# Two small jobs change engines: the columns of ones of the reused weight tiles, and the first chunk's casts

## The chip, the cores and the metric

The kernel runs on one core of a Trainium2 chip. A core has five engines with a queue each: TensorE (PE in the profile, with its weight loads as PEld), VectorE (DVE), ScalarE (ACT), GpSimd (POOL) and SyncE (SP), which here only issues transfers. They run beside each other and meet through semaphores. The metric is the time of one execution in microseconds (us), the median of several runs.

## The reference

Four batches of eight heads, 768 tokens, head width 64. Queries and keys are hashed by six random projections into 64 buckets, and a query attends only to keys of its own bucket. The heads' outputs, side by side, are the 512-wide rows of a feed-forward layer with three branches of which the largest value is kept.

```python
q_bits = (np.einsum('bhsd,dk->bhsk', q, proj) > 0).astype(np.int64)
k_bits = (np.einsum('bhsd,dk->bhsk', k, proj) > 0).astype(np.int64)
...
mask = q_bucket[:, :, :, None] == k_bucket[:, :, None, :]
scores = scale * np.matmul(q, k.transpose(0, 1, 3, 2))
scores = np.where(mask, scores, -1000000000.0)
scores = scores - np.max(scores, axis=-1, keepdims=True)
attn = np.exp(scores)
attn = attn / (np.sum(attn, axis=-1, keepdims=True) + 1e-09)
...
x = np.ascontiguousarray(attn_out.transpose(0, 2, 1, 3)).reshape(B * S, H * D)
...
h = np.maximum(np.maximum(x @ w1, x @ w2), x @ w3)
return (h @ w_out).astype(np.float32)
```

Inputs and outputs are float32.

## The kernel before

**Chunks and units.** The queries of a batch are cut into chunks: three of 256 queries in the first batch, two of 384 in each of the others, nine in all. A unit is one step of the attention: for one chunk and one head, as many blocks of 128 keys as give 768 score columns, so three blocks of 256 queries in the first batch and two of 384 later. Each batch has 48 units, the kernel 192. For a unit TensorE computes scores from S, a tile with the scaled heads and, below them, the hash bits as plus or minus one half (L299). ScalarE then takes one exponential over all 768 columns (L307) into a weight tile AT; its bias lets only equal hashes through. The scores lie in one of two buffers in PSUM, so TensorE can start the scores of a unit only when the exponential of the unit two before it has ended.

**Weight tiles.** There are 29 AT tiles, handed out first in, first out (`at_free`). A tile holds its blocks side by side, and behind each block's columns stand two columns of ones, which let the matmul with the values give the sum of the values as one column more. Their place depends on the block's width: the tiles start in the 256-wide form, with ones written by VectorE (L531). When a unit of the second batch takes a tile that is still in that form, `scores` lets VectorE write the new ones in front of the exponential:

```python
        if at_form[i] != w:
            nc.vector.memset(t[:, :, w : w + 2], 1.0)
            at_form[i] = w
```

That is L305. Tiles that the first batch's chunks give back for heads 4 to 7 (`i == 1`) have theirs written by GpSimd when they are given back (L396), at the end of a burst.

**Bursts.** When four heads of a chunk are done, a burst multiplies the weights with a matrix of ones (L359, the sums) and with the values (L381, one matmul group for each half of the value columns), with transposes and a reciprocal of the sums on VectorE (L366 to L370) and the scaled result into the chunk's xT (L388). From the fourth chunk on, VectorE first adds the blocks (L330, L333) and the sums of eight heads are taken at once (L414).

**Feed-forward groups.** When a chunk's xT is whole, its feed-forward work is put in a list and handed out one piece for each unit, behind that unit's scores: a group of four matmuls (L447) for one of three branches and one of six column blocks. The first branch's result is cast out of PSUM into ht by ScalarE (L451); the other two are folded in by VectorE with a maximum (L453). In the first chunk all six casts come first, in six groups one after another; in later chunks a cast comes with every third group. At the end come the output matmuls (L488) and their copies by ScalarE (L492). All these, the hash and the bursts share four PSUM banks, taken and given back in turn.

**Preparation.** The heads of the later batches are transposed on VectorE in blocks of 32 (L203), narrowed by GpSimd (L208), and written into S by transfers that SP issues (L213); their hash is computed by TensorE (L222), turned into bits by VectorE (L225) and sent to S by SP (L233). GpSimd also issues transfers: weights (L249, wout in L246), values (L241), and heads (L197).

**Order.** Nothing is rearranged: each engine executes its instructions in the order in which the program issues them. One loop over the units issues in each turn the scores of the next unit, the preparation that is planned for that turn (`when`), a piece of feed-forward work if there is credit, and the bursts that are due. The memset of L305 is issued with the scores, so on VectorE it stands behind everything of the turns before.

Of the kernel before, what the change touches and what calls it, by code (L numbers as in the profile page):

```python
# [17 lines left out]
def kernel(  # L18
# [12 lines left out]
    nc = tc.nc  # L31
# [59 lines left out]
    def bank():  # L91
        i = free_banks.pop(0)
        return i, bank_tiles[i]

    def give(i):
        if i is not None:
            free_banks.append(i)
# [168 lines left out]
    UPB = NU // B  # L266
# [4 lines left out]
    at_free = list(range(NAT))  # L271
    at_form = [THIRD] * NAT
    at_of = {}
# [6 lines left out]
    def block_of(b, m):  # L280
        return 2 * (m % MH) + m // MH if b == 0 else m
# [29 lines left out]
    def weights_of(c, h, m):  # L311
        w = chunks[c][2]
        nb = 2 * HALF // w
        return blocks(at_tiles[at_of[unit_at[c, h, m // nb]]], w)[:, m % nb, :]

    def xt_of(c):
        if c not in xts:
            xts[c] = x_pool.tile([P, NJC, HALF], FP16, tag="xT", name="xT")
        return xts[c]
# [15 lines left out]
    def sum_blocks(c, h):  # L335
        w = chunks[c][2]
        if (c, h) in sum_of:
            t = sum_of[c, h]
            return [t[:, j, 0:w] for j in range(1 if c >= THIRD_ADD else 2)]
        return [weights_of(c, h, m)[:, 0:w] for m in range(NM)]  # L340

    def burst(c, i):
        b, q0, w = chunks[c]
        held = {}
        rb = []

        def own_bank(key):
            if c == NCH - 1 and i == 1 and key != 1:
                return None, sc_ps.tile([P, 2, 512], FP32, tag="sc", name="sc")[:, 0, :]
            return bank()  # L350

        def sums(m0, m1):
            if m0 == 0:
                held["s"] = own_bank("s")
            sm = held["s"][1]
            bs = [sum_blocks(c, 4 * i + x) for x in range(4)]
            for m in range(len(bs[0])):
                for x in range(4):
                    nc.tensor.matmul(sm[Q * x : Q * (x + 1), 0:w], ones[:, :], bs[x][m],  # L359
                                     start=(m == 0), stop=(m == len(bs[0]) - 1))  # L360
            if m1 == NM:
                ys = ys_pool.tile([P, HALF], FP32, tag="ys", name="ys")
                rr = small.tile([P, HALF // Q], FP32, tag="rr", name="rr")
                n = w // Q
                rb.append(rb_pool.tile([P, HALF], FP32, tag="rb", name="rb"))
                nc.vector.transpose(ys[:, 0:w], sm[:, 0:w])  # L366
                give(held["s"][0])
                nc.vector.tensor_scalar(out=rr[:, 0:n], in0=ys[:, 0:w:Q], scalar1=EPS * S, scalar2=None, op0=AluOp.add)
                nc.vector.reciprocal(rr[:, 0:n], rr[:, 0:n])
                nc.vector.transpose(rb[0][:, 0:w], rr[:, 0:n].unsqueeze(2).to_broadcast((P, n, Q)))  # L370

        def values(side, m0, m1):
            if m0 == 0:
                held[side] = own_bank(side)
            av = held[side][1]
            first = (b, i, side) not in sv_of
            n = w + 1 if first else w
            for m in range(m0, m1):
                cb = block_of(b, m)
                for x in range(4):  # L380
                    nc.tensor.matmul(av[Q * x : Q * (x + 1), 0:n], v_at[2 * b + i][:, x, cb * D + side : (cb + 1) * D : 2],  # L381
                                     weights_of(c, 4 * i + x, m)[:, 0:n], start=(m == 0), stop=(m == NM - 1))
            if m1 == NM:
                if first:
                    sv_of[b, i, side] = small.tile([P, 1], FP32, tag=f"sv{side}", name="sv")
                    nc.vector.tensor_scalar(out=sv_of[b, i, side][:], in0=av[:, w : w + 1], scalar1=EPS, scalar2=None,
                                            op0=AluOp.mult)
                nc.vector.scalar_tensor_tensor(out=xt_of(c)[:, 2 * i + side, 0:w], in0=av[:, 0:w],  # L388
                                               scalar=sv_of[b, i, side][:], in1=rb[0][:, 0:w], op0=AluOp.add, op1=AluOp.mult)
                give(held[side][0])  # L390
                if side == 1:
                    for h in range(4 * i, 4 * i + 4):
                        for n in range(parts_of(c)):
                            a = at_of[unit_at[c, h, n]]
                            if b == 0 and i == 1:
                                nc.gpsimd.memset(blocks(at_tiles[a], HALF)[:, :, HALF : HALF + 2], 1.0)  # L396
                                at_form[a] = HALF
                            at_free.append(a)

        return sums, values, rb  # L400


# [33 lines left out]
    def ffn_groups(c):  # L436
        b, q0, w = chunks[c]
        xt = xt_of(c)
        hts, gs, l2 = {}, [], {}
        jobs = [(fb, wi) for fb in range(NFB) for wi in range(3)]  # L440
        if c == 0:
            jobs = [(fb, wi) for wi in range(3) for fb in range(NFB)]
        for fb, wi in jobs:
            def go(fb=fb, wi=wi):
                k_, ps = bank()
                for jc in range(NJC):
                    nc.tensor.matmul(ps[:, 0:w], w_sb[wi][:, jc, fb * P : (fb + 1) * P], xt[:, jc, 0:w],  # L447
                                     start=(jc == 0), stop=(jc == NJC - 1))
                if wi == 0:
                    hts[fb] = h_pool.tile([P, HALF], FP16, tag="ht", name="ht")  # L450
                    nc.scalar.copy(hts[fb][:, 0:w], ps[:, 0:w])  # L451
                else:
                    nc.vector.tensor_tensor(out=hts[fb][:, 0:w], in0=hts[fb][:, 0:w], in1=ps[:, 0:w], op=AluOp.max)  # L453
                give(k_)
            gs.append(go)
        rows = out[b * S : (b + 1) * S, :].rearrange("(p c) m -> c p m", c=NM)

        def out_rows(tb):
            if c < NCH - 1:
                return o_pool.tile([P, DM], FP32, tag="osb", name="osb")  # L460
            if "end" not in nat:
                nat["end"] = nat_pool.tile([P, 4 * NM * D], FP32, tag="nat", name="nat")
            return nat["end"][:, tb * DM : (tb + 1) * DM]

        def last(tb, cs, use_act):
            k_, ps = bank()
            n = cs.stop - cs.start
            for fb in range(NFB):
                nc.tensor.matmul(ps[:, 0:n], hts[fb][:, tb * P : (tb + 1) * P], wout_sb[:, fb, cs],  # L469
                                 start=(fb == 0), stop=(fb == NFB - 1))  # L470
            osb = out_rows(tb)
            if use_act:
                nc.scalar.copy(osb[:, cs], ps[:, 0:n])
            else:
                nc.vector.tensor_copy(osb[:, cs], ps[:, 0:n])
            give(k_)
            (nc.scalar if use_act else nc.sync).dma_start(rows[block_of(b, q0 // P + tb)][:, cs], osb[:, cs])

        def item(tb, part):
            def go2(part, tb=tb):  # L480
                if c == NCH - 1 and tb == w // P - 1:
                    last(tb, slice(part * DM // 2, (part + 1) * DM // 2), part == 0)
                    return
                if part == 0:
                    l2[tb] = bank()
                k_, ps = l2[tb]
                for fb in range(part * MH, (part + 1) * MH):
                    nc.tensor.matmul(ps[:, 0:DM], hts[fb][:, tb * P : (tb + 1) * P], wout_sb[:, fb, :],  # L488
                                     start=(fb == 0), stop=(fb == NFB - 1))
                if part == 1:  # L490
                    osb = out_rows(tb)
                    nc.scalar.copy(osb[:, 0:DM], ps[:, 0:DM])  # L492
                    give(k_)
                    nc.sync.dma_start(rows[block_of(b, q0 // P + tb)], osb[:, 0:DM])
            gs.append(lambda: go2(part))

        ntb = w // P
        steps = [(0, 0)]
        for tb in range(1, ntb):
            steps += [(tb, 0), (tb - 1, 1)]  # L500
        steps.append((ntb - 1, 1))
        if c == NCH - 1:
            steps = steps[:-3] + [steps[-2], steps[-3], steps[-1]]
        for tb, part in steps:
            item(tb, part)
        return gs
# [202 lines left out]
```

## Time and profile before

| What | Value |
|---|---|
| Median of 3 runs | 265.15 us (264.85 to 265.51) |
| The profiled execution | 264.99 us, of which 262.8 us from the first to the last instruction |
| TensorE, matmuls | 256.1 us busy, 97% |
| VectorE | 199.2 us busy, 76% |
| ScalarE | 180.7 us busy, 69% |
| GpSimd | 69.9 us busy, 27% |
| L305, memsets of ones on VectorE | 5, 62 ns each, from 55.5 to 62.2 us |
| L396, memsets of ones on GpSimd | 24, 102 ns each, from 41.1 to 60.7 us |
| L451, casts on ScalarE | 54: 18 of 128x256 (401 ns), 36 of 128x384 (481 ns) |

Times of instructions are counted from the first instruction of the profiled execution. In a row of a group, the line number and the engine come first, then what is written and read with its shape; behind the bar stand the total busy time, the mean duration of one in ns, and the idle time of the engine just before these instructions with what ended it. In a timeline row the start and the duration come first. Instructions of one engine overlap in part, so a row's duration is longer than its share of the engine's time. TensorE's ends are modelled.

### The profile page before, as it was taken

What the parts mean: (1) busy time and instruction counts of PE and PEld (TensorE: products, weight loads), DVE (VectorE), ACT (ScalarE), POOL (GpSimd) and SP (SyncE); (2) the same over time, 40 slices, a digit from 0 to 9 for tenths busy, and PEclk for the clock granted to TensorE, in tenths of its full rate; (3) what the DMA queues carried; (4) which work ended last, traced back from release to release, by engine and by line L of the source; (5) the groups of instructions that cost most, each with busy time, mean ns of one, the idle gap of its engine ahead of it and who ended that gap; (6) DMA issues with size and microseconds to landing.
All of it is one profiled execution on the core that took longest, in us unless ns stands there. A gap on an engine that the chain in (4) does not pass through costs nothing.

```text
span 262.8 us, 6491 instructions
## 1 busy us (share of the span) xinstructions
PE 256.1 (97%) x2503; PEld 155.8 (59%) x2503; DVE 199.2 (76%) x472; ACT 180.7 (69%) x276; POOL 69.9 (27%) x132
## 2 busy tenths in 40 slices
PE   7999999999999999999999999999999999999995
PEld 3655657765675676556555555556555555555552
DVE  3897757567598799769989899799847895888360
ACT  3797876765999199935898278981898739581322
POOL 3868753274067017400162412110000000000000
PEclk9999999999999999999999999999999999999999
DMA  7996999979446826950064851900230003000303
GB/s 216 339 243 141 173 238 225 204 158 219 143 113 185 159 64 111 240 159 12 0 180 122 163 94 40 199 4 18 59 121 2 0 2 120 2 1 2 120 0 120
DMA packets 20717, 30.95 MB, mean 118 GB/s; under 512 B 2608, under 2 KB 15248, under 8 KB 20688
## 3 DMA queue, kind: packets, MB, share of 16 engines
q0 software_dynamic: 8128, 13.37, 26.7%
q1 hardware_dynamic: 12128, 16.66, 21.7%
q10 hardware_dynamic: 432, 0.52, 0.6%
q8 instruction: 19, 0.31, 0.5%
q14 instruction: 10, 0.08, 0.1%
HBM read 25.17 MB, written 6.29 MB: 120 GB/s over the span
## 4 chain that ended last, share of the span: by engine, by line
PE 90%; ACT 7%; issue 1%; DVE 0%; ACTq 0%
PE ms L447 34%; PE sc L299 23%; PE ms L381 11%; PE ms L488 11%; ACT AT L307 5%; PE ms L222 3%; PE ms L359 2%; PE ms L124 1%; PE ms L538 1%; PE ms L172 1%; PE ms L414 1%; ACT ht L451 1%; PE ms L151 1%; PE ms L469 1%; PE sc L381 0%
## 5 line engine op out<-in xcount | busy, mean ns | idle before, releaser
L307 ACT ACTIVATE AT<-sc 128x768 f16<-128x768 f32 x192 | 153.1, 822 | 55.7 <-PE sc L299 52.7
L447 PE MATMUL ms<-xT,w_sb 128*128 128x384 f16 (+1 forms) x648 | 115.0, 308 | 0.2 <-DVE xT L388 0.2
L299 PE MATMUL sc<-S 72*128 72x384 bf16 (+1 forms) x432 | 93.7, 308 | 1.9 <-ACT AT L307 1.3
L447 PEld LDWEIGHTS <-w_sb 128*128 128x128 f16 x648 | 62.8, 97 | 35.6
L453 DVE TENSOR_TENSOR ht<-ht,ms 128x384 f16<-128x384 f16 (+1 forms) x108 | 54.2, 504 | 34.4 <-PE ms L447 21.9
L299 PEld LDWEIGHTS <-S 72*128 72x128 bf16 (+1 forms) x432 | 39.9, 98 | 32.2 <-issue 11.4
L208 POOL TENSOR_SCALAR T<-T 128x768 bf16<-128x768 f32 x24 | 22.8, 952 | 85.1 <-issue 51.5
L488 PE MATMUL ms<-wout_sb,ht 128*128 128x512 f16 x138 | 35.5, 378 | 0.0
L381 PE MATMUL ms<-AT,vo 128*32 128x385 f16 (+3 forms) x840 | 33.4, 308 | 0.0
L451 ACT CAST ht<-ms 128x384 f16<-128x384 f32 (+1 forms) x54 | 24.5, 454 | 8.8 <-PE ms L447 8.8
L381 PEld LDWEIGHTS <-vo 128*32 128x32 f16 x864 | 23.6, 96 | 8.5 <-issue 1.3
L330 DVE TENSOR_TENSOR ad<-ad,AT 128x768 f16<-128x768 f16 x48 | 26.9, 560 | 2.2 <-ACT AT L307 1.5
L330 DVE TENSOR_TENSOR ad<-AT,AT 128x768 f16<-128x768 f16 x48 | 27.7, 578 | 0.2 <-ACT AT L307 0.2
L203 DVE STREAM_TRANSPOSE T<-nat 128x384 f32<-128x384 f32 x48 | 26.5, 562 | 0.0
L488 PEld LDWEIGHTS <-ht 128*128 128x128 f16 x138 | 13.3, 97 | 13.0 <-issue 0.3
L388 DVE SCALAR_TENSOR_TENSOR xT<-ms,sv,rb 128x384 f16<-128x384 f32 (+1 forms) x35 | 19.1, 563 | 1.1
L492 ACT COPY osb<-ms 128x512 f32<-128x512 f32 x21 | 12.3, 588 | 6.1 <-issue 5.0
L333 DVE TENSOR_TENSOR ad<-ad 128x384 f16<-128x384 f16 x32 | 15.5, 484 | 1.1
L138 POOL TENSOR_SCALAR S<-T 64x384 bf16<-64x384 f32 (+1 forms) x23 | 14.1, 616 | 4.7 <-DVE T L133 3.1
L197 POOL DMA_DIRECT2D nat<-in_q_dram x20 | 11.1, 559 | 0.5 <-issue 0.4
L177 DVE TENSOR_SCALAR S<-ms 6x384 bf16<-6x384 f32 x16 | 8.9, 554 | 2.0 <-PE ms L172 1.2
L197 POOL DMA_DIRECT2D nat<-in_k_dram x16 | 9.0, 570 | 0.4
(60 smaller groups left out, 109.9 us busy)
## 6 DMA issues: line engine op xcount, KB each, us to landing
out_dram<-osb SPq DMA_DIRECT2D x21, 256.0 KB
S<-T SPq DMA_DIRECT2D x48, 96.0 KB
nat<-in_q_dram POOLq DMA_DIRECT2D x20, 192.0 KB, 5.9
vo<-in_v_dram POOLq DMA_DIRECT2D x8, 384.0 KB, 7.8
nat<-in_k_dram POOLq DMA_DIRECT2D x16, 192.0 KB, 4.2
w_sb<-in_moe_w_dram POOLq DMA_DIRECT2D x3, 768.0 KB, 10.2
nat<-in_k_dram SPq DMA_DIRECT2D x10, 192.0 KB
nat<-in_k_dram SPq DMA_DIRECT2D x3, 384.0 KB
```

The source lines that it names most:

```text
L197: eng.dma_start(dst, src)
L203: nc.vector.transpose(t32[name][:, u, half * HALF : (half + 1) * HALF], i_)
L208: nc.gpsimd.tensor_scalar(out=t16[name][:, u, :], in0=t32[name][:, u, :], scalar1=RS, scalar2=1.0, op0=AluOp.mult, op1=AluOp.mult)
L299: nc.tensor.matmul(views[j], s_of[kn][0 : D + bits, kx, m * P : (m + 1) * P], s_of[qn][0 : D + bits, qx, q0 : q0 + w], start=True, stop=True)
L307: nc.scalar.activation(t[:, :, 0:w], whole, ActFn.Exp, bias=-SCALE * 0.25 * bits, scale=SCALE)
L330: nc.vector.tensor_tensor(out=sum_of[c, h][:], in0=t[0], in1=t[n], op=AluOp.add)
L381: nc.tensor.matmul(av[Q * x : Q * (x + 1), 0:n], v_at[2 * b + i][:, x, cb * D + side : (cb + 1) * D : 2], weights_of(c, 4 * i + x, m)[:, 0 ...
L388: nc.vector.scalar_tensor_tensor(out=xt_of(c)[:, 2 * i + side, 0:w], in0=av[:, 0:w], scalar=sv_of[b, i, side][:], in1=rb[0][:, 0:w], op0=A ...
L447: nc.tensor.matmul(ps[:, 0:w], w_sb[wi][:, jc, fb * P : (fb + 1) * P], xt[:, jc, 0:w], start=(jc == 0), stop=(jc == NJC - 1))
L451: nc.scalar.copy(hts[fb][:, 0:w], ps[:, 0:w])
L453: nc.vector.tensor_tensor(out=hts[fb][:, 0:w], in0=hts[fb][:, 0:w], in1=ps[:, 0:w], op=AluOp.max)
L488: nc.tensor.matmul(ps[:, 0:DM], hts[fb][:, tb * P : (tb + 1) * P], wout_sb[:, fb, :], start=(fb == 0), stop=(fb == NFB - 1))
```

## The change

Two edits that touch each other in no line.

The first moves memsets of ones. A tile that the first batch gives back gets its columns of ones for the 384-wide form from GpSimd if the unit that will take it belongs to the second batch. The program knows this when the tile is given back: the tiles handed out so far (`at_of`, which keeps every unit) and those free in front of it (`at_free`) are counted, and if they are 48 or more the next to take this tile is in the second batch. Before, the rule was that the tile came from heads 4 to 7. The 24 tiles that GpSimd already wrote keep their place; five more, given back by heads 0 to 3 of the third chunk, join them, and VectorE's five memsets go.

The second moves the first chunk's six casts from ScalarE to VectorE.

```diff
                             a = at_of[unit_at[c, h, n]]
-                            if b == 0 and i == 1:
+                            if b == 0 and len(at_of) + len(at_free) >= UPB:
                                 nc.gpsimd.memset(blocks(at_tiles[a], HALF)[:, :, HALF : HALF + 2], 1.0)
                                 at_form[a] = HALF
                             at_free.append(a)
...
                     hts[fb] = h_pool.tile([P, HALF], FP16, tag="ht", name="ht")
-                    nc.scalar.copy(hts[fb][:, 0:w], ps[:, 0:w])
+                    if c:
+                        nc.scalar.copy(hts[fb][:, 0:w], ps[:, 0:w])
+                    else:
+                        nc.vector.tensor_copy(hts[fb][:, 0:w], ps[:, 0:w])
                 else:
                     nc.vector.tensor_tensor(out=hts[fb][:, 0:w], in0=hts[fb][:, 0:w], in1=ps[:, 0:w], op=AluOp.max)
```

On TensorE the order of the instructions stays as it was. On GpSimd the five memsets stand between the two L208 that narrow the queries of the first four heads of the second batch, in front of the transfer of wout (L246). On VectorE the first three casts stand ahead of four L203 (keys of the last four heads of the second batch), the other three between them.

## The prediction

> **What bounds the kernel now.** I read the page first: busy time by engine, then the granted clock.
>
> ```profile
> PE 256.1 (97%) x2503; PEld 155.8 (59%) x2503; DVE 199.2 (76%) x472; ACT 180.7 (69%) x276; POOL 69.9 (27%) x132
> PEclk9999999999999999999999999999999999999999
> ```
>
> TensorE is busy in 256.1 of 262.8 us at full granted clock, and 262.8 - 256.1 = 6.7 us is all that it idles, start and end included. So an edit that adds or removes no matmul can gain only where the in-order stream of matmuls is held up, and those places must be found one by one. Its ends are modelled, so I go by starts. Next I read the chain of work that ended last in the stretch that the edits touch (start, duration, what). Almost everywhere it runs through PE rows; these are places where it leaves them:
>
> ```profile
> 43.24 0.38 ACT ht L451
> 43.61 0.40 ACT AT L307
> ...
> 45.57 0.72 ACT AT L307
> 46.29 0.27 ACT ht L451
> 46.55 0.72 ACT AT L307
> ...
> 61.43 0.82 ACT AT L307
> 62.25 0.04 issue
> 62.29 0.48 PE sc L299 x2
> ```
>
> From 43.2 to 47.3 it alternates on ScalarE between an exponential (L307) and a cast (L451): the first chunk's casts. At 61.43 it is one exponential that TensorE waits for. The table of stretches (stretch, length, busy time of PE, PEld, DVE, ACT and POOL, clock, DMA share, GB/s) compares the first place with a stretch with the same matmuls and no casts on ScalarE:
>
> ```profile
> 43.46:47.32 3.86, 3.70 (x31) 2.70 (x28) 0.94 (x3) 3.86 (x10) 0.82 (x1) 1.00 1.21 236
> 50.27:54.88 4.61, 4.61 (x46) 4.09 (x43) 4.48 (x12) 4.01 (x6) 3.08 (x11) 1.00 0.57 120
> ```
>
> The reader is to see ACT at 3.86 of 3.86 us in the first, with DVE at 0.94. In the second PE is full and ACT has room. Each holds units of three 256-wide score matmuls followed by a group of four 256-wide FFN matmuls. The first runs four such pairs in 3.86 us, starts at 43.46, 44.38, 45.36, 46.34 and 47.32; the second six in 4.61 us, 0.768 each. Last, the timeline around the second place (start, duration, engine, line, operation, idle before with its releaser):
>
> ```profile
> 60.41 0.88 DVE L388 SCALAR_TENSOR_TENSOR xT<-ms,sv,rb 128x256 f16<-128x256 f32 x2
> ...
> 60.91 0.49 PE L299 MATMUL sc<-S 72*128 72x384 bf16 x2
> ...
> 61.22 0.41 DVE L453 TENSOR_TENSOR ht<-ht,ms 128x256 f16<-128x256 f16 x1
> 61.24 0.40 DVE L305 MEMSET AT<- 128x4 f16 x2
> 61.24 0.60 PE L447 MATMUL ms<-xT,w_sb 128*128 128x256 f16 x4
> 61.43 3.02 ACT L307 ACTIVATE AT<-sc 128x768 f16<-128x768 f32 x4 [2.61 <-PE sc L299]
> ...
> 62.29 0.48 PE L299 MATMUL sc<-S 72*128 72x384 bf16 x2 [0.45 <-ACT AT L307]
> ```
>
> The scores of one unit start at 60.13. Elsewhere the exponential starts 0.60 us after its scores (50.27 and 50.87), so 60.73; here 61.43. The row names PE as releaser, but PE had long been done: in the order of VectorE the tile's memset (L305) stands behind the two L388, which end near 61.29. The score buffers are two, so the next scores but one start at 62.29, not at 61.67, which is 60.91 plus 0.76 (the spacing of the next pair, 62.29 to 63.05).
>
> **The change part by part.** *Casts.* Six 128x256 casts leave ScalarE (L451, 401 ns each, some 0.25 us of the cycle, since instructions overlap) and enter VectorE, each in front of that unit's max. ScalarE then runs the exponentials alone. Back to back they start every 0.745 us (five in 3.79 us from 35.00: (3.79 - 0.81) / 4), below the 0.768 us of TensorE, so the four pairs take 4 x 0.768 = 3.07 us: 3.86 - 3.07 = 0.79 us gained on the path. The buffers allow it: scores at 44.23 need the exponential of those at 42.70; that one starts at 43.30 (0.60 later), ends 0.81 on at 44.11, and the release takes about 0.06. [...]
>
> What a cast costs on VectorE no row shows. Below: 385 ns, the mean L453 of this width between 50.2 and 55 us. Above: 553 ns, the L133 copy out of PSUM at 384 columns. Nearest: the one L475 copy of 128x256 f32 at 425 ns, which I take. In a queue it is less: a stream transpose (L203) and an L453 together repeat every 0.79 us (51.93, 52.73, 53.51). In the new order three casts come first, at the pace of TensorE, then transpose and cast alternate four times to the first L453. I lay that out from 42.54, where L388 ends: third cast done near 44.9, fourth 45.8, sixth 47.4, last transpose 47.85, first L453 48.25. TensorE needs the fourth cast's bank for the sums at 48.17 - 0.79 = 47.38 and the sixth's for the second values near 48.8, so 1.4 us to spare. Even at 553 ns, 0.13 more for each of six, 0.8 in all, that margin holds. If the cover went, VectorE would delay the sums' L366 (then about 48.35) and its lateness would count one to one beyond about 1.0 us. So: nothing on the path. The four transposes slip by some 3.5 us; GpSimd's first L208 that reads them moves from 43.57 to about 46.4 and ends before the memsets of 50.12, behind which the second stands anyway, and SP's next writes of S begin at 51.84. Covered.
>
> *Ones.* Five L305 memsets of 62 ns leave VectorE, and five L396 memsets enter GpSimd: 24 become 29. The other 24 stay where they were. The second place then closes: the exponential at 60.73, ending 61.54, frees the buffer in time for 61.67; 62.29 - 61.67 = 0.62 us gained. What is late next is TensorE itself: the following units (63.05, 64.03, 65.00) are spaced by their own matmuls. The other two late exponentials (55.62, 58.01) are followed by sixteen L222 and by 72 L359 and L381 matmuls, so they gain nothing; as an outer bound, 0.17 us of idle time before the first and 58.01 - 57.77 = 0.24 before the second.
>
> On GpSimd the five stand behind the first of two L208 that start at 35.22 and 36.54, and wait for the values at 35.16 on TensorE, which end by 36.0. The rows for L396:
>
> ```profile
> L396 POOL MEMSET AT<- 128x4 f16 x24 | 1.7, 102 | 11.6 <-PE ms L381 11.3 <-PE sc L299 0.3
> ```
>
> Seven of them run in 0.45 us, so five take 0.33; the outer bound is each with its own 0.33 us wait and 0.10 us duration, 2.15 us. Started at 36.05, they end at 36.4 (then the second L208, ready near 36.5, loses about 0.1) or at 38.2 (1.7 lost). Queued behind it: the issue of wout (37.42, landing in 13.4 us, wanted at 63.38), a V load, and on SP the last four S<-T and four S<-bits. Those must land before the second batch's first scores, 54.88 - 0.79 = 54.09. The view of DMA between 45 and 55 us, in 40 slices of 0.25 us, shows when:
>
> ```profile
> DMA  9999999999999999999999999542100047566475
> GB/s 238 248 248 272 260 252 252 260 252 250 256 288 255 260 240 208 207 226 292 253 206 215 209 244 172 114 86 65 18 9 0 0 74 154 154 129 191 129 172 141
> ```
>
> The queues run empty at 52.5, so at least 1.6 us remain, which the 0.1 I take does not touch and the outer 1.7 barely does. TensorE has no other wait on a transfer: its granted stream from 75 to 200 us is busy throughout, so the gain passes to the end.
>
> **The sum.** 0.79 + 0.62 = 1.41 us. The profiled execution took 264.99 us (span 262.8, 2.2 around it), which gives 263.58. The median of the runs is 265.15, 0.16 above; from it 263.74. I forecast 263.7.
>
> **The rivals.**
> - *VectorE takes ScalarE's place as the bound in the cast stretch.* For it: DVE is at 4.48 of 4.61 us in the comparable stretch. Against: that stretch still kept 0.768. If all 0.79 is lost, 265.15 - 0.62 = 264.53.
> - *Only the casts pay*: the exponential at 60.73 is held by something else that also ended near 61.4, which the wrong releaser in its row leaves possible. 265.15 - 0.79 = 264.36.
> - *The work is hidden*, both gaps reopen a unit later, as ScalarE is on the chain again at 65.59 to 69.1 with two output copies: 265.15. Against: ScalarE was idle before 64.61 and 65.59, so nothing is carried into that place.
> - *Slower: GpSimd's queue.* A memset that waits for TensorE holds the L208 behind it. For it: the L208 at 50.98 ran right behind memsets, though its transposes had ended by 44.4. [...] If the L208 at 36.54 slips by more than 1.6 + 1.41 = 3.0 us, the late S costs more than is won; the longest wait of an L396 is 5.7 us, with which the time is 265.15 + 5.7 - 3.0 = 267.8. Against: here the values end at 36.0, just as the first L208 ends.
>
> **How the numbers follow.** Both gaps 0.72, casts only 0.08, ones only 0.07, hidden 0.07, slower 0.06. About 0.3%, 0.8 us, is what a measurement can tell from no change. Faster takes both gaps and most of casts only, which lies at the line: 0.78. Same takes the rest of it, ones only and hidden: 0.16. Slower 0.06. The range begins at 263.2, which is 263.74 less 0.41 for the outer bound of the exponentials at 55.62 and 58.01, less 0.1 for ScalarE's spacing, and ends at 264.6, which takes in either part alone.
>
> **What would show it.** Right: the starts of L299 from 43.46 on spaced by 0.77 us, no L451 row of chunk 0 on ACT, ACT with idle time between exponentials; the L299 behind the third unit of batch two without its 0.45 us wait; 29 L396 rows, none of L305; the second L208 near 36.6. Wrong: a wait of L447 or L359 for VectorE between 44 and 52, a wait of L299 for S near 54, or an exponential after 60 us that still starts over 0.7 us after its scores.

## The result and the profile after

The changed kernel takes 263.32 us (median of four runs, 263.26 to 263.52) against 265.14 us before: a ratio of 0.9928, 95% interval 0.9911 to 0.9944. Measured twice more beside the kernel before, it came to 0.9942 (0.9929 to 0.9954) and 0.9943 (0.9929 to 0.9957). The three gains are 1.82, 1.47 and 1.29 us; the forecast was 1.41, that is 263.7 us.

First the page of the changed kernel, its line of busy time by engine:

```profile
PE 255.8 (98%) x2503; PEld 156.3 (60%) x2503; DVE 201.2 (77%) x473; ACT 179.4 (69%) x270; POOL 70.5 (27%) x137
```

VectorE is busy 2.0 us longer, ScalarE 1.3 us less, and the matmuls are the same 2503. Next the chain of work of the changed kernel where the casts were (start, duration, what). Exponentials and casts of ScalarE stood here in turn; now only TensorE does:

```profile
44.54 0.33 PE sc L299 x3
44.87 0.44 PE ms L447 x4
45.31 0.33 PE sc L299 x3
45.64 0.44 PE ms L447 x4
```

The table of stretches (stretch, length, busy time of PE, PEld, DVE, ACT and POOL, clock, DMA share, GB/s) shows the same four pairs of scores and FFN group in the changed kernel, from 43.61 to 46.68:

```profile
43.61:46.68 3.07, 3.07 (x30) 2.72 (x28) 2.53 (x7) 3.07 (x5) 0.31 (x1) 1.00 1.23 227
```

They take 3.07 us where they took 3.86. TensorE is now full there, and VectorE has gone from a quarter of the time to 2.53 of 3.07 us. ScalarE still reads as full, because successive exponentials overlap: each lasts 0.81 us, and from 43.43 on they start 0.71 to 0.77 us apart. The starts of the scores, 0.77 us apart, show that it no longer sets the pace.

Then the timeline of the changed kernel around the second place (start, duration, engine, line, operation, idle before with its releaser):

```profile
59.51 0.50 PE L299 MATMUL sc<-S 72*128 72x384 bf16 x2
...
59.79 0.88 DVE L388 SCALAR_TENSOR_TENSOR xT<-ms,sv,rb 128x256 f16<-128x256 f32 x2
59.84 0.60 PE L447 MATMUL ms<-xT,w_sb 128*128 128x256 f16 x4
60.10 3.11 ACT L307 ACTIVATE AT<-sc 128x768 f16<-128x768 f32 x4 [2.15 <-POOL AT L396]
...
60.28 0.49 PE L299 MATMUL sc<-S 72*128 72x384 bf16 x2
...
61.05 0.49 PE L299 MATMUL sc<-S 72*128 72x384 bf16 x2
```

The exponential starts 0.59 us after its scores, no longer 1.30, and L388 on VectorE runs past its start without holding it. The third scores follow the second after 0.77 us, with no wait. The releaser named for the exponential, an L396 on GpSimd, can't be a cause: the ones of this tile were written near 36 us, and the start is the usual 0.6 us after the scores.

Between the two traces every matmul can be set against itself. The differences of their starts change in three places and nowhere else: at the very start of the kernel, +0.15 us by the scores at 8.84; from 43.46 to 47.32, -0.79; at 62.29, -0.61. From there to the last matmul the shift is constant. The last group of L469 shows it whole (here in the kernel before at 258.17, in the changed one at 256.93, 1.24 apart, where 0.79 + 0.61 - 0.15 is 1.25):

```profile
256.93 1.47 PE L472 MATMUL ms<-wout_sb,ht 128*128 128x256 f16 x12
```

The rest of the first comparison lies at the edges: the kernel before had 2.2 us outside its span in the profiled execution, the changed one 1.8. No term of the prediction has this 0.4 us; the repeats below show that it is no chance.

### The profile page after: what moved, and what is told of

It reads as the page before. It is cut to its first block, busy times and chain, and to the rows that moved or that the text cites. A ratio compares the mean times of both kernels' runs of the same rounds, so it can differ in the third digit from the quotient of the medians.

```text
span 261.5 us, 6493 instructions
## 1 busy us (share of the span) xinstructions
PE 255.8 (98%) x2503; PEld 156.3 (60%) x2503; DVE 201.2 (77%) x473; ACT 179.4 (69%) x270; POOL 70.5 (27%) x137
## 4 chain that ended last, share of the span: by engine, by line
PE 92%; ACT 5%; DVE 1%; issue 1%; ACTq 0%
PE ms L447 35%; PE sc L299 23%; PE ms L491 11%; PE ms L381 11%; ACT AT L307 4%; PE ms L222 3%; PE ms L359 2%; PE ms L124 1%; PE ms L172 1%; PE ms L541 1%; PE ms L414 1%; PE ms L151 1%; ACT T L131 1%; PE ms L472 1%; DVE xT L388 0%
## 5 line engine op out<-in xcount | busy, mean ns | idle before, releaser
L208 POOL TENSOR_SCALAR T<-T 128x768 bf16<-128x768 f32 x24 | 22.9, 954 | 86.7 <-issue 50.9
L452 ACT CAST ht<-ms 128x384 f16<-128x384 f32 (+1 forms) x48 | 21.8, 454 | 8.8 <-PE ms L447 8.8
L203 DVE STREAM_TRANSPOSE T<-nat 128x384 f32<-128x384 f32 x48 | 26.8, 564 | 0.0
L388 DVE SCALAR_TENSOR_TENSOR xT<-ms,sv,rb 128x384 f16<-128x384 f32 (+1 forms) x35 | 19.1, 563 | 1.1
```

The source lines that it names most:

```text
L203: nc.vector.transpose(t32[name][:, u, half * HALF : (half + 1) * HALF], i_)
L208: nc.gpsimd.tensor_scalar(out=t16[name][:, u, :], in0=t32[name][:, u, :], scalar1=RS, scalar2=1.0, op0=AluOp.mult, op1=AluOp.mult)
```

## The experiments

**Each edit alone, and both again.** The first experiment keeps the old rule for the ones:

```diff
-                            if b == 0 and len(at_of) + len(at_free) >= UPB:
+                            if b == 0 and i == 1:
```

> The first chunk's six casts go to VectorE, the columns of ones stay as in the kernel before. Theory (two separate gaps that add): the scores between 43.5 and 47.3 us are spaced 0.77 us instead of 0.98, 0.79 us are gained there, and the wait of 0.45 us of L299 near 62 us stays: 265.14 - 0.79 = 264.35 us. Rival (one edit carries the whole 1.82 us, or what lies outside the span belongs to one edit): under 263.9 us, or 265.1 us.

Measured: 264.45 against 265.20 us, ratio 0.9973 (0.9963 to 0.9983). Its timeline keeps the second place as it was:

```profile
59.95 0.49 PE L299 MATMUL sc<-S 72*128 72x384 bf16 x2
...
60.27 0.40 DVE L305 MEMSET AT<- 128x4 f16 x2
...
60.44 3.02 ACT L307 ACTIVATE AT<-sc 128x768 f16<-128x768 f32 x4 [2.61 <-PE sc L299]
...
61.30 0.49 PE L299 MATMUL sc<-S 72*128 72x384 bf16 x2 [0.43 <-ACT AT L307]
```

The second keeps the casts on ScalarE:

```diff
-                    if c:
-                        nc.scalar.copy(hts[fb][:, 0:w], ps[:, 0:w])
-                    else:
-                        nc.vector.tensor_copy(hts[fb][:, 0:w], ps[:, 0:w])
+                    nc.scalar.copy(hts[fb][:, 0:w], ps[:, 0:w])
```

> GpSimd writes the five tiles' ones at the give-back, the casts stay on ScalarE. Theory (two separate gaps): the scores between 43.5 and 47.3 us stay spaced 0.98 us, the wait of L299 near 62 us goes, 0.62 us gained: 265.14 - 0.62 = 264.52 us. Rival (one edit carries all): 263.3 or 265.1 us. If e1 and e2 together gain clearly less than the whole change, what is left over belongs to neither gap.

Measured: 264.39 against 265.20 us, ratio 0.9963 (0.9951 to 0.9976). In its table of stretches the four pairs keep their old length, with ScalarE as the full engine, while the timeline of TensorE has the later scores without a wait:

```profile
44.13:47.99 3.86, 3.70 (x31) 2.70 (x29) 0.93 (x3) 3.86 (x10) 0.82 (x1) 1.00 1.20 239
```

```profile
60.80 0.50 PE L299 MATMUL sc<-S 72*128 72x384 bf16 x2
...
61.58 0.49 PE L299 MATMUL sc<-S 72*128 72x384 bf16 x2
...
62.34 0.49 PE L299 MATMUL sc<-S 72*128 72x384 bf16 x2
```

Set against the trace of before, e1 gains 0.79 us at the casts alone and e2 0.61 at 62.29 alone. The two gaps are separate and add. That also settles the rival by which only one of them would pay. The medians alone wouldn't show it so well: e2's is 0.81 us below the kernel before and not 0.61, for a reason that comes next.

> The changed kernel once more, beside the two halves. Theory: 1.40 us of the gain lie in the two gaps, and what the first measurement showed above it (1.82 - 1.40 = 0.42 us) is scatter of the start and the end of an execution: between 1.2 and 1.9 us below the kernel before. Rival (the surplus is real): again 1.8 us below, with the time outside the span again 1.8 instead of 2.2 us.

Measured: 263.73 against 265.20 us, ratio 0.9942 (0.9929 to 0.9954). Its trace has the same two steps, -0.79 and -0.60. A third measurement was made beside a later version:

> The changed kernel once more, beside the version with the second chunk's casts on VectorE. Theory: the trace keeps the two gaps closed (1.40 us), and the rest is scatter of the start and of the time outside the span, so the gain is between 1.2 and 1.9 us.

Measured: 263.69 against 264.98 us, ratio 0.9943 (0.9929 to 0.9957). Both gains lie in the expected range, but scatter is only half of the account. The start of an execution scatters: by the scores near 9 us the profiled executions lie -0.2 to +0.8 us from that of the kernel before, although nothing there was changed (in the two repeats 0.3 us later). The time outside the span does not. Wherever an execution's span is on record, its time less the span is 2.2 to 2.3 us in the kernel before, in e1 and in e7 below, and 1.7 to 1.9 us in the ten other runs. The first three are those in which VectorE writes the five tiles' ones; e2 differs from the kernel before in that edit alone, and e7 from the changed kernel. So some 0.43 us outside the span go with the edit of the ones, and to that extent the rivals of e1 and e3, by which the surplus belongs to one edit and is real, were right. In the repeats later starts ate most of it: the median span fell by about 0.95 and 0.9 us, not by 1.40. One other row of the pages differs in the same way, that of a DMA queue of the kind "instruction". It has ten packets in those three kernels (here the kernel before) and eleven in the ten others (here the changed kernel):

```profile
q14 instruction: 10, 0.08, 0.1%
q14 instruction: 11, 0.09, 0.1%
```

Whether the two belong together no run shows, nor what else sets the time outside the span.

**Was it the engine or the place in the order?** VectorE writes the five tiles' ones after all, but at the give-back:

```diff
-                                nc.gpsimd.memset(blocks(at_tiles[a], HALF)[:, :, HALF : HALF + 2], 1.0)
+                                eng = nc.gpsimd if i == 1 else nc.vector
+                                eng.memset(blocks(at_tiles[a], HALF)[:, :, HALF : HALF + 2], 1.0)
```

> The changed kernel, but VectorE writes the five tiles' ones, at the same give-back: the same engine as before the change, 25 us earlier in its order. Theory (the place in the order made the wait, not the engine): the scores near 61 us keep no wait, and five memsets of 62 ns at 36 us cost nothing: within 0.15 us of the changed kernel. Rival (VectorE's time was what mattered): 0.3 to 0.6 us slower than the changed kernel.

Measured: 264.00 against 265.16 us, ratio 0.9952 (0.9940 to 0.9965). That is some 0.3 us above the changed kernel's repeats, more than the 0.15 of the theory, though the intervals overlap. The trace shows where it isn't: the five memsets cost VectorE 0.11 us at a time when it waits anyway for L222,

```profile
37.09 0.11 DVE L397 MEMSET AT<- 128x4 f16 x5
39.70 0.56 DVE L225 TENSOR_SCALAR bits<-ms 128x384 bf16<-128x384 f32 x1 [2.50 <-PE ms L222]
```

and the three scores start at 59.75, 60.52 and 61.29, without a wait. From the scores near 9.8 us to the end it loses 0.07 us against the changed kernel. So the place in the order made the wait, and GpSimd was one way to another place. The engine counts outside the span alone, where e7 has the 2.2 us of the kernel before.

**VectorE's margin.** Each cast of the first chunk is made twice:

```diff
-                        nc.vector.tensor_copy(hts[fb][:, 0:w], ps[:, 0:w])
+                        for _ in range(2):
+                            nc.vector.tensor_copy(hts[fb][:, 0:w], ps[:, 0:w])
```

> The changed kernel with each of the six casts made twice on VectorE. Theory of the prediction (VectorE's casts are covered until it is about 1.0 us late at the sums): each second cast adds 0.31 to 0.39 us to a pair that took 0.79, so VectorE is about 1.4 us late at the transpose of the sums (L366, 48.44 in the changed kernel), and 0.2 to 0.6 us reach the end: 263.5 to 263.9 us. Rival (VectorE was already the bound of this stretch): all of it counts, 1.4 us or more, 264.7 us and later.

Measured: 263.95 against 265.16 us, ratio 0.9955 (0.9940 to 0.9971), just above the theory's 263.9 us. The timeline of VectorE, and TensorE's main new wait:

```profile
43.14 2.46 DVE L455 CAST ht<-ms 128x256 f16<-128x256 f32 x6 [0.36 <-PE ms L447]
...
48.51 0.84 DVE L455 CAST ht<-ms 128x256 f16<-128x256 f32 x2
49.27 0.57 DVE L203 STREAM_TRANSPOSE T<-nat 128x384 f32<-128x384 f32 x1
49.77 0.38 DVE L457 TENSOR_TENSOR ht<-ht,ms 128x256 f16<-128x256 f16 x1
50.07 0.43 DVE L366 STREAM_TRANSPOSE ys<-ms 128x256 f32<-128x256 f32 x1
```

```profile
49.41 0.85 PE L381 MATMUL ms<-AT,vo 128*32 128x256 f16 x24 [0.26 <-DVE ht L455]
```

L366 starts at 50.07, where it was at 48.44 in the changed kernel: 1.5 us late, allowing for 0.1 us of a later start. At the second values TensorE has lost 0.44 us, at a later group 0.06 more: 0.50 of the 1.5 us pass to the end. VectorE was not the bound; the cover is about 1 us at the transpose. TensorE meets the lateness earlier, at the bank of the sixth cast: that pair ends 1.9 us later than the one cast did and costs 0.44, so some 1.4 us were to spare there, as the prediction laid out.

**GpSimd's queue.** The slower rival is forced, by writing the same ones 15 times:

```diff
-                                nc.gpsimd.memset(blocks(at_tiles[a], HALF)[:, :, HALF : HALF + 2], 1.0)
+                                for _ in range(1 if i == 1 else 15):
+                                    nc.gpsimd.memset(blocks(at_tiles[a], HALF)[:, :, HALF : HALF + 2], 1.0)
```

> The changed kernel with each of the five new memsets on GpSimd made 15 times, 75 in place of 5: at 0.064 us each the L208 behind them slips by about 4.5 us. Theory (S of the second batch lands 1.6 us before it is wanted): TensorE waits for S near 54 us, and 4.5 - 1.6 = 2.9 us are lost, 266.2 us. Rival (the transfers are held by the DMA queues, not by GpSimd, so the slip is absorbed there): under 0.5 us lost, 263.3 to 263.8 us.

Measured: 271.74 against 265.16 us, ratio 1.0251 (1.0237 to 1.0265), some 8 us above the changed kernel. Both expectations missed, first of all because the repeats take 11.49 us and not 4.8. Its rows on GpSimd and on TensorE:

```profile
36.59 11.49 POOL L397 MEMSET AT<- 128x4 f16 x75
48.17 0.83 POOL L208 TENSOR_SCALAR T<-T 128x768 bf16<-128x768 f32 x1
```

```profile
60.89 0.80 PE L299 MATMUL sc<-S 72*128 72x384 bf16 x2 [6.15 <-issue]
61.48 1.06 PE L448 MATMUL ms<-xT,w_sb 128*128 128x256 f16 x4
62.47 2.40 PE L222 MATMUL ms<-T,pj 128*32 128x384 f32 x16
```

The L208 behind them slips by 11.2 us, and the second batch's first scores by 6.3 (both less the 0.3 us of a later start). S<-bits, the last part of these scores' input, goes out on SP from 52.10 on, where it was 46.23 in the changed kernel: 5.6 us late, again less the later start. So the mechanism is real, but 4.9 us of the slip are covered. A smaller dose, 6 in place of 15, was to tell a fixed cover from the 1.6 us of the prediction:

> The changed kernel with each of the five new memsets made 6 times, 30 in place of 5. Repeats on one tile came 0.153 us apart in the run with 75, so they take 4.6 us and the L208 behind them slips by 4.3. In the run with 75 a slip of 11.2 us cost 6.3 us at the scores near 54 us. Theory A (a fixed cover: 11.2 - 6.3 = 4.9 us): nothing is lost, within 0.2 us of the changed kernel, 263.3 to 263.9 us. Theory B (the cover of the prediction, 1.6 us): 2.7 us lost at the scores near 54 us, 266 us and later.

Measured: 263.26 against 265.07 us, ratio 0.9933 (0.9919 to 0.9947): nothing is lost. On GpSimd the L208 moved from 36.69 to 40.62, and every matmul starts within 0.04 us of the changed kernel's:

```profile
36.25 4.29 POOL L397 MEMSET AT<- 128x4 f16 x30
40.62 0.86 POOL L208 TENSOR_SCALAR T<-T 128x768 bf16<-128x768 f32 x1
```

SP's timeline explains the cover. Of its eight S<-T in this stretch the first four can't need that L208: in e6 they go out by 42.3, before it runs. The fifth starts almost at the same time in the changed kernel (first row) and in e8 (second), and 6.0 us later in e6 (third), again less the later start:

```profile
42.69 0.54 SPq L213 DMA_DIRECT2D S<-T  x1
42.87 0.54 SPq L213 DMA_DIRECT2D S<-T  x1
49.03 0.54 SPq L213 DMA_DIRECT2D S<-T  x1
```

In the changed kernel the L208 ends at 37.52, 5.2 us before that transfer is issued. SP's longest waits from 34 to 47 us there (first row) are put down to earlier loads, while in e6 (34 to 53 us, second row) SP waits for the L208 itself:

```profile
SPq L213 <- DMA nat<-in_k_dram: 5.4, 4, 3.6
SPq L213 <- POOL T L208: 6.4, 1, 6.4
```

GpSimd was 3.9 us late in e8, and S<-bits behind these transfers still goes out at 46.23, as in the changed kernel; the rows leave room for about 5 us.

**Further in the same direction.** ScalarE stays on the chain a little later, where the chain of the changed kernel reads:

```profile
65.06 0.87 ACT osb L495 x2
...
66.07 0.62 ACT AT L307
...
66.77 0.38 ACT ht L452
67.15 0.73 ACT AT L307
...
67.92 0.48 PE sc L299 x2
```

First the first chunk's two output copies were moved:

```diff
-                    nc.scalar.copy(osb[:, 0:DM], ps[:, 0:DM])
+                    if c:
+                        nc.scalar.copy(osb[:, 0:DM], ps[:, 0:DM])
+                    else:
+                        nc.vector.tensor_copy(osb[:, 0:DM], ps[:, 0:DM])
```

> The changed kernel, and the first chunk's two output copies (128x512) also go from ScalarE to VectorE, which is idle for 3.1 us there. Theory (ScalarE is late after those two copies): the scores at 67.92 us lose their 0.22 us, and 0.1 to 0.2 us of the two later ones: 0.2 to 0.45 us faster than the changed kernel, about 263.0 us. Rival (ScalarE is the bound of the next units by its casts alone, three exponentials and a cast taking 2.49 us where TensorE needs 2.30): the gap only moves to a later unit, and the time stays within 0.1 us.

Measured: 263.75 us beside 263.73 for the changed kernel in the same comparison. In the trace the wait at 67.92 shrinks by 0.10 us, those of 0.13 at the two later scores stay, and two waits near 93 and 97 us grow by 0.06 each. The time is the rival's; of the theory's 0.22 us half went. That the casts, one in every third unit, are what holds the scores there is the rival's reason, and the next two runs test it. Three of the second chunk's casts were moved instead:

```diff
-                    if c:
+                    if c > 1 or (c == 1 and fb % 2):
```

> The changed kernel, and three of the six casts of the second chunk go to VectorE as well. Theory A (ScalarE still holds the scores there, 0.22 + 0.13 + 0.13 us in the rows from 67.9 to 74.7): these waits go, 0.3 to 0.5 us faster than the changed kernel, about 263.0 us. Theory B (VectorE, with additions and transposes back to back from 67 us on, has no room there and becomes late itself): L447 waits for VectorE's banks, and the time is the same or up to 0.5 us slower.

Measured: 263.09 us, ratio 0.9931 (0.9917 to 0.9944). Against the changed kernel's trace it gains 0.21 us, all at the scores that were at 67.92, whose cast had moved; the two waits of 0.13 belong to casts that hadn't. Then all six:

```diff
-                    if c:
+                    if c > 1:
```

> The changed kernel with all six casts of the second chunk on VectorE as well. In the run with three of them the wait of 0.22 us at the first cast went and the two of 0.13 us stayed, at casts that were still ScalarE's. Theory A: these two go as well, 0.48 us faster than the changed kernel in the trace, about 263.0 us. Theory B (VectorE has no room left from 67 us on): waits of L447 for VectorE's banks appear between 68 and 80 us and take back 0.3 us or more.

Measured: 263.73 us beside 263.69 for the changed kernel. Both theories hold, one after the other: the three waits go, 0.47 us in the trace, and then TensorE waits for VectorE, which takes back 0.45 us in one place and 0.07 in another, all that was won:

```profile
79.15 0.60 PE L447 MATMUL ms<-xT,w_sb 128*128 128x256 f16 x4 [0.28 <-DVE ht L456]
```

The version with three casts moved is the best trace of all, but its 0.2 us can't be told from the changed kernel by the times.

## Why the prediction was right

*Both gaps, 0.79 + 0.62.* Measured 0.79 and 0.61 in the traces, and each alone in e1 and e2. The pace of the new stretch was read from a stretch with the same matmuls, and the exponentials keep TensorE's pace of 0.77 us. The two other late exponentials gained nothing, as forecast: between 47.32 and 62.29 the starts keep their difference.

*The cast on VectorE, taken at 425 ns and no cost on the path.* The row of the changed kernel reads 406 ns:

```profile
L454 DVE CAST ht<-ms 128x256 f16<-128x256 f32 x6 | 2.4, 406 | 1.1 <-PE ms L447 1.1
```

The order laid out ahead was met to 0.1 us: the sixth cast ends at 47.38, the last transpose at 47.86, the first max ends at 48.16, L366 starts at 48.44. The prediction also says that each cast enters "in front of that unit's max"; that doesn't fit its own layout, in which all six stand in front of the first max, as they do. The slip of GpSimd's L208 to 46.37 cost nothing. The rival with VectorE as the bound falls: e5 shows 1 to 1.4 us of room.

*The memsets on GpSimd.* Five took 0.33 us, as taken, and the L208 behind them lost nothing beyond the later start.

*The slower rival.* Its chance was small for the right reason, but its size was wrong. The step "at least 1.6 us remain" counted only the time between the landing of S and its use; it left out that SP stands behind its own earlier transfers. The cover is between 3.9 us (e8, no loss) and 4.9 (e6), if it is one number for both, and the 5.2 us in SP's rows agree. With 1.41 us to lose, it would have needed a slip of some 6 us, not of 3.0, to make the kernel slower. The 1.6 us themselves gave no cover in e6: S<-T went out 6.0 us late and the scores started 6.3 late. Why is open.

*The rest of 1.82.* The sum left the 2.2 us around the span as they were. That was wrong: it is 1.8 us in the changed kernel, a gain of some 0.43 us that no term foresaw. The two gaps, 1.40 us in the traces, fit the 1.41 by their mechanism. That two of the three times, 1.47 and 1.29 us below the kernel before, come near it as well is partly luck: there the 0.43 us and a later start cancel. Whether the later start belongs to the change isn't shown.

## What to carry to other kernels

On a kernel whose matmul engine is full, look along its stream for the stretches where equal work is spaced unequally: the spacing of the undisturbed stretch prices the gain, here to 0.02 us. A small instruction costs what stands in front of it in its queue (one memset of 62 ns cost 0.61 us here), so issue it when the tile it writes is free and not when that tile is needed; for the wait, which engine took it made no difference (in e7, with VectorE, the three scores start 0.77 us apart as well). And look at the time outside the span of each run: what looks like scatter can belong to a kernel. Work moved to a half-idle engine pays until that engine's backlog outlasts the free buffers, and the next six casts showed that point within one chunk (e10: 0.47 us won, 0.52 taken back).

## What the runs showed of the hardware

After the wait of 6 us in e6 TensorE ran at a lower granted clock, in the table of stretches of e6:

```profile
54.00:60.80 6.80, 0.74 (x7) 0.40 (x5) 1.03 (x3) 1.15 (x2) 3.97 (x7) 0.76 1.22 212
60.80:64.80 4.00, 3.91 (x22) 1.32 (x22) 0.42 (x1) 0.81 (x1) 0.00 (x0) 0.56 1.23 182
64.80:70.00 5.20, 5.20 (x100) 4.05 (x97) 3.94 (x11) 2.42 (x4) 1.77 (x11) 1.00 1.02 213
```

The sixteen L222 took 2.40 us instead of 1.50, and the slow stretch cost 1.6 us on top of the wait. The granted clock is 1.00 from 46.0 to 54.0 us, 0.76 on average from 54.0 to 60.8, where the wait lies, 0.50 in each of the three microseconds from 60.8 to 63.8, 0.73 in the next, and 1.00 from 64.8. What lowers and restores it no run shows.

Memsets of 128x4 on GpSimd took about 0.06 us each on different tiles (0.45 us for seven, where one alone lasts 0.10) and 0.15 us each where they repeat on the same tile (11.49 us for 75, 4.29 for 30). Why a repeat takes longer no run shows.
